# Turning a projection through the DMA crossbar instead of TensorE, and splitting the last store, in a Linformer attention and max-out feed-forward kernel

## Chip, cores, metric

One core of one Trainium2 chip. The metric is the device time of one execution in microseconds (us), the median of several; most executions of a kernel agree within 0.3%.

## The reference, cut to what matters

```python
# q, k, v: (batch 8, heads 8, seq 1024, head_dim 64); E, F: (64, 1024)
k_proj = np.einsum('ks,bhsd->bhkd', E, k)        # 64 x 64 per head
v_proj = np.einsum('ks,bhsd->bhkd', F, v)
scores = q @ k_proj.transpose(0, 1, 3, 2) / 8    # then softmax over 64
attn_out = softmax(scores) @ v_proj
x = attn_out.transpose(0, 2, 1, 3).reshape(8192, 512)
out = np.maximum(x @ w1, x @ w2) @ w_out         # w1, w2: 512 x 1024; w_out: 1024 x 512
```

The feed-forward part is computed with Strassen-like products, two units of seven products per batch. The attention of batch b is laid between the products of batch b-1, at numbered slots (14 per batch).

## The kernel before

Each engine works off its instructions in program order and waits on semaphores; the scheduler inserts the waits. kp is k's projection (64 x 64 per head) and kpt its transpose, which the scores need; "to turn" is to transpose, and "through the crossbar" means by `dma_start_transpose`.

```python
def step_kv(t, h0=0, h1=H, which="kv", att=False):     # k's and v's projection: 16 matmuls (L180)
    kv_ps = att_banks()[:, 0, :] if att else mm_bank()
    ...
    eng(out=fl(t["kp"]), in_=kv_ps[0:KP, 0:n])                              # ACT
    ...
    nc.vector.tensor_copy(out=fl(t["vp"][KP:128]), in_=kv_ps[KP:128, 0:n])
    nc.vector.tensor_copy(out=fl(t["vp"][0:KP]), in_=kv_ps[KP:128, 0:n])

def step_kpt(t, h0=0, h1=H, att=False):                # each head turned twice, to rows 0-63 and 64-127
    kpt_ps = att_banks(FP16)[:, 0, :] if att else mm_bank(FP16)
    for h in range(h0, h1):
        for r in range(2):
            nc.tensor.transpose(out=kpt_ps[r * D : (r + 1) * D, ...], in_=t["kp"][:, h, :], ...)
    nc.vector.tensor_copy(out=t["kpt"][:, h0:h1, :]..., in_=kpt_ps[...])

def step_qt_dma(t, h0=0, h1=H):                        # q is turned by the crossbar already
    nc.sync.dma_start_transpose(out=t["qt"][:, h0:h1]..., in_=t["q"][:, h0:h1]...)

def load(t, n, src, b, h0, h1, c0=0, c1=NC):           # float32 in HBM to 16 bits in SBUF
    nc.gpsimd.dma_start(out=t[n][...], in_=src[b, h0:h1]...)
...
# batches 3 to 7; step_sc (scores) reads kpt and qt
at(b - 1, -11, 0, new_attn, t)
at(b - 1, -11, 0, step_qt_dma, t, 0, H // 2)
at(b - 1, -11, 0, step_qt_dma, t, H // 2, H)
at(b - 1, -9, 0, step_kv, t, 0, H, "kv", True)
at(b - 1, -9, 0, loads, b + 1, "v", "q", "k")
at(b - 1, -8, 0, step_kpt, t, 0, H, True)
plan = "sc0 -7, da0 -6, sc1 -4, da1 -3, sc2 -1, da2 0, sc3 2, da3 3"
```

k, q and v share four buffers, so the next loads wait until the q transposes and the projection have freed three of them.

The softmax here doesn't subtract the row's maximum and nothing guards it: scores larger than these inputs give would overflow.

## Time and profile before

| | before |
|---|---|
| time, median | 347.74 us (3 runs), 347.49 us (4 runs, beside the changed kernel) |
| span of the profiled run | 345.4 us |
| TensorE busy, clock granted | 96%, 0.996 |
| projection to projection, batches 3 to 7 | 37.94 us |
| last matmul's end to the end of the span | 4.9 us |

The first row is the metric; the others are from one profiled execution. The period is read from the first matmul of the projection (line L180) of successive batches. The lines of the page are in the prediction.

### The profile page before, as it was taken

To read this page: it belongs to the slowest core of one execution; us is meant where nothing else is said; L and a number is where in the kernel's file an instruction comes from. 1 tells how busy PE (TensorE), PEld (TensorE's weight loads), DVE (VectorE), ACT (ScalarE), POOL (GpSimd) and SP (SyncE) were. 2 spreads that over 40 slices of the span, in tenths; PEclk is the share of its full clock that TensorE was granted. 3 is DMA by queue.
4 is the path that set the end of the run, shared out by engine and by line. 5 is a ranking of instruction groups with operands and counts; after the bars stand their busy time and mean duration, and the time that the engine had idled before them with its cause. 6 is when DMAs were issued, how large, how long until landed. Compare 5 with 4: busy or idle time off the path is not lost.

```text
span 345.4 us, 7094 instructions
## 1 busy us (share of the span) xinstructions
PE 332.9 (96%) x2979; PEld 233.5 (68%) x2979; DVE 232.4 (67%) x394; ACT 218.7 (63%) x325; POOL 31.5 (9%) x43
## 2 busy tenths in 40 slices
PE   8988999999999999999999999999999999999994
PEld 4543444434476777777777777777777777888883
DVE  1367717534787778686769778686869777777561
ACT  2437222773896778668884777668875788654541
POOL 8433002011103000120012000100000000000000
PEclk9999999999999999999999999999999999999998
DMA  8999999999998999799669949891923030303033
GB/s 154 200 197 201 207 207 193 238 159 260 174 205 183 195 208 250 109 191 193 173 114 181 222 122 172 150 200 20 199 47 123 2 121 2 121 5 123 0 123 121
DMA packets 65232, 52.36 MB, mean 152 GB/s; under 512 B 26160, under 2 KB 56880, under 8 KB 65200
## 3 DMA queue, kind: packets, MB, share of 16 engines
q0 software_dynamic: 31312, 28.31, 53.7%
q1 hardware_dynamic: 33888, 23.60, 25.2%
q8 instruction: 23, 0.38, 0.4%
q14 instruction: 9, 0.07, 0.1%
HBM read 57.15 MB, written 16.78 MB: 214 GB/s over the span
## 4 chain that ended last, share of the span: by engine, by line
PE 75%; DVE 9%; ACT 6%; DMA 6%; POOL 2%; issue 1%; DVEq 0%; ACTq 0%; POOLq 0%
PE mm_ps L630 31%; PE mm_ps L552 21%; PE mm_ps L385 5%; DMA big<-in_moe_w_dram 4%; PE mm_ps L359 4%; PE att_ps L265 4%; PE att_ps L180 3%; DVE big L496 2%; PE att_ps L241 2%; DVE xt_sb L279 2%; ACT ld_sb L272 2%; DVE gt_sb L567 2%; PE mm_ps L425 2%; ACT ld_sb L275 2%; PE mm_ps L520 2%
## 5 line engine op out<-in xcount | busy, mean ns | idle before, releaser
L506 ACT COPY p_sb<-mm_ps 128x512 f32<-128x512 f32 x160 | 89.1, 592 | 44.0 <-PE mm_ps L630 29.6
L630 PEld LDWEIGHTS <-big 128*128 128x128 f16 x672 | 65.7, 98 | 8.1 <-DVE big L496 0.5
L630 PE MATMUL mm_ps<-T_sb,big 128*128 128x256 f16 x504 | 61.6, 273 | 0.3 <-DVE big L496 0.3
L279 DVE TENSOR_TENSOR xt_sb<-att_ps,ld_sb 128x1024 f16<-128x1024 f32 x28 | 34.2, 1221 | 29.2 <-ACT ld_sb L275 29.1
L567 DVE TENSOR_TENSOR gt_sb<-mm_ps,p_sb 128x512 f16<-128x512 f32 x52 | 35.8, 689 | 22.4 <-PE mm_ps L552 22.4
L552 PEld LDWEIGHTS <-big 128*128 128x128 f16 x416 | 38.9, 98 | 12.7 <-issue 8.5
L552 PE MATMUL mm_ps<-big 128*128 128x256 f16 x312 | 43.7, 273 | 0.3 <-DVE gt_sb L567 0.3
L552 PEld LDWEIGHTS <-wd_sb 128*128 128x128 f16 x312 | 28.2, 98 | 13.8 <-issue 10.7
L630 PEld LDWEIGHTS <-gt_sb 128*128 128x128 f16 x336 | 32.7, 98 | 4.2 <-DVE gt_sb L570 0.2
L630 PE MATMUL mm_ps<-wo_sb,gt_sb 128*128 128x256 f16 x224 | 33.7, 273 | 0.0
L552 PE MATMUL mm_ps<-xt_sb,wd_sb 128*128 128x256 f16 x208 | 31.0, 273 | 2.3 <-DVE gt_sb L567 2.3
L249 ACT ACTIVATE ex_sb<-att_ps 128x1024 f16<-128x1024 f32 x28 | 28.9, 1031 | 4.2 <-PE att_ps L241 4.2
L272 ACT ACTIVATE ld_sb<-att_ps 128x1024 f32<-128x1024 f32 x28 | 28.9, 1030 | 3.5 <-PE att_ps L265 3.5
L275 ACT ACTIVATE ld_sb<-ld_sb 128x1024 f32<-128x1024 f32 x28 | 30.0, 1070 | 0.4
L646 DVE TENSOR_TENSOR o_sb<-mm_ps,p_sb 128x512 f32<-128x512 f32 x28 | 19.3, 689 | 12.1 <-PE mm_ps L630 12.1
L630 PE MATMUL mm_ps<-m_sb,xt_sb 128*128 128x256 f16 x112 | 21.4, 273 | 0.0
L102 POOL DMA_DIRECT2D v_sb<-in_v_dram x9 | 7.7, 863 | 145.1 <-DMA qt_sb<-q_sb 120.8
L570 DVE TENSOR_SCALAR gt_sb<-gt_sb 128x512 f16<-128x512 f16 (+1 forms) x52 | 19.1, 367 | 1.8
L496 DVE TENSOR_TENSOR big<-gt_sb 128x1024 f16<-128x1024 f16 x28 | 19.2, 685 | 0.9
L602 ACT ACTIVATE gt_sb<-mm_ps 128x512 f16<-128x512 f32 x26 | 15.6, 599 | 4.7 <-PE mm_ps L552 4.7
L630 PEld LDWEIGHTS <-xt_sb 128*128 128x128 f16 x168 | 16.4, 98 | 1.9
L567 DVE TENSOR_TENSOR gt_sb<-p_sb 128x512 f16<-128x512 f32 x26 | 17.7, 681 | 0.0
(94 smaller groups left out, 455.4 us busy)
## 6 DMA issues: line engine op xcount, KB each, us to landing
out_dram<-o_sb SPq DMA_DIRECT2D x28, 512.0 KB, 3.1
k_sb<-in_k_dram POOLq DMA_DIRECT2D x7, 1024.0 KB, 18.2
v_sb<-in_v_dram POOLq DMA_DIRECT2D x7, 1024.0 KB, 9.9
q_sb<-in_q_dram POOLq DMA_DIRECT2D x7, 1024.0 KB, 13.6
big<-in_moe_w_dram POOLq DMA_DIRECT2D x8, 256.0 KB, 14.3
out_dram<-o_sb SPq DMA_DIRECT2D x8, 256.0 KB, 4.6
k_sb<-in_k_dram POOLq DMA_DIRECT2D x2, 512.0 KB, 7.8
v_sb<-in_v_dram POOLq DMA_DIRECT2D x2, 512.0 KB, 12.5
```

What stands on the lines that cost most here:

```text
L249: nc.scalar.activation(out=ex, in_=sc_ps, func=ACTF.Exp, scale=scale)
L272: nc.scalar.activation(out=ld, in_=dn_ps, func=ACTF.Ln)
L275: nc.scalar.activation(out=ld, in_=ld, func=ACTF.Exp, scale=-1.0)
L279: nc.vector.tensor_tensor(out=t["xt"][:, p, :, :], in0=at_ps, in1=ld, op=ALU.mult)
L385: nc.tensor.matmul(out=op_ps, lhsT=lhsT, rhs=rhs, start=(n == 0), stop=(n == NFB + NDC - 1),)
L496: nc.vector.tensor_tensor(out=S(i), in0=x, in1=y, op=op)
L506: nc.scalar.copy(out=x, in_=bank)
L552: nc.tensor.matmul(out=bank[:, m * W : (m + 1) * W], lhsT=w_[:, n_, (2 * d + m) * 128 : (2 * d + m + 1) * 128], rhs=a[:, n_, :], start=(n ...
L567: nc.vector.tensor_tensor(out=c_blk(j, c), in0=two(x), in1=two(y), op=ALU.add)
L570: nc.vector.tensor_scalar_max(ap, ap, 0.0)
L630: nc.tensor.matmul(out=bank[:, i * CH : (i + 1) * CH], lhsT=a(c)[:, i * 128 : (i + 1) * 128], rhs=w_(c), start=(n is not None and i == 0 a ...
L646: nc.vector.tensor_tensor(out=cols(st["o", j], c), in0=two(x), in1=two(y), op=ALU.add)
```

## The change

Intent: free TensorE of the 16 small transposes per batch by sending kp through the DMA crossbar, with the projection moved a slot earlier to give the DMA time; and shorten the end by storing the last tile in small pieces as they become ready. Core of the diff (line numbers shift: L180 stays, L229 becomes L242, L241 L254, L630 L643, L650 L663):

```diff
-        t["kp"] = proj.tile([KP, H, D], FP16, tag="kp", name="kp_sb")
+        t["kp"] = proj.tile([KP, H, 2, D], FP16, tag="kp", name="kp_sb")
...
+            def finish_v():                         # runs after the next slot
+                nc.vector.tensor_copy(out=fl(t["vp"][KP:128]), in_=kv_ps[KP:128, 0:n])
+                if att:
+                    nc.vector.tensor_copy(out=kp[:, :, 1, :], in_=kp[:, :, 0, :])
+                    step_kpt_dma(t)
+                nc.vector.tensor_copy(out=fl(t["vp"][0:KP]), in_=fl(t["vp"][KP:128]))
...
+    def step_kpt_dma(t):
+        nc.sync.dma_start_transpose(
+            out=t["kpt"], in_=t["kp"].rearrange("p h r d -> p (h r d)")
+        )
...
         def p4():
+            if alone:                               # the last unit of the program
+                for i in range(2):
+                    bank = product(4, ("C", i), 2 + i, (i,))
+                    ...add u2 on DVE...
+                    store(1, i, i + 1, 0, CH)       # 128 KB each; p3 has stored the other half
+                return
...
-            at(b - 1, -11, 0, new_attn, t)          # and both step_qt_dma
-            at(b - 1, -9, 0, step_kv, t, 0, H, "kv", True)
-            at(b - 1, -9, 0, loads, b + 1, "v", "q", "k")
-            at(b - 1, -8, 0, step_kpt, t, 0, H, True)
+            at(b - 1, -12, 0, new_attn, t)          # and both step_qt_dma
+            at(b - 1, -9 if b == 3 else -10, 2 if b == 3 else 0, step_kv, t, 0, H, "kv", True)
+            at(b - 1, -7, 0, loads, b + 1, "v", "q", "k")
+            if b == 3:
+                plan = "sc0 -5, da0 -4, sc1 -3, da1 -2, sc2 -1, da2 0, sc3 2, da3 3"
```

More of the change, by code (lines that the diff above doesn't have):

```diff
@@ L188, in step_kv @@
             eng = nc.vector.tensor_copy if which == "k" else nc.scalar.copy
-            eng(out=fl(t["kp"]), in_=kv_ps[0:KP, 0:n])
+            kp = t["kp"][:, h0:h1]
+            eng(out=kp[:, :, 0, :], in_=kv_ps[0:KP, 0:n].rearrange("p (h d) -> p h d", d=D))
         if both:
@@ L192, in step_kv, with step_kpt @@
         elif "v" in which:
-            nc.vector.tensor_copy(out=fl(t["vp"][KP:128]), in_=kv_ps[KP:128, 0:n])
-            nc.vector.tensor_copy(out=fl(t["vp"][0:KP]), in_=kv_ps[KP:128, 0:n])
-    def step_kpt(t, h0=0, h1=H, att=False):
-        kpt_ps = att_banks(FP16)[:, 0, :] if att else mm_bank(FP16)
+            def finish_v():
[4 more added lines that the diff above has]
+                nc.vector.tensor_copy(out=fl(t["vp"][0:KP]), in_=fl(t["vp"][KP:128]))
+            return finish_v
+    def step_kpt(t, h0=0, h1=H):
+        kpt_ps = mm_bank(FP16)
         for h in range(h0, h1):
@@ L202, in step_kpt @@
                     out=kpt_ps[r * D : (r + 1) * D, (h - h0) * KP : (h - h0 + 1) * KP],
-                    in_=t["kp"][:, h, :],
+                    in_=t["kp"][:, h, 0, :],
                     identity=ident16[:KP, :KP],
@@ L610, in cat, with product @@
             return lambda n: g[:, n] if n < NG else x[:, n - NG]
-        def product(k, name, n):
+        def product(k, name, n, part=(0, 1)):
             if n is not None:
@@ L627, in product @@
             }[k]()
-            for i in range(2):
+            for i in part:
                 for c in range(NG + NX):
@@ L633, in product @@
                         rhs=w_(c),
-                        start=(n is not None and i == 0 and c == 0),
+                        start=(n is not None and i == part[0] and c == 0),
                         stop=(c == NG + NX - 1), skip_group_check=True,
@@ L647, in add, with store @@
                 out=cols(st["o", j], c), in0=two(x), in1=two(y), op=ALU.add)
-        def store(j):
+        def store(j, i0=0, i1=2, m0=0, m1=DM):
             nc.sync.dma_start(
                 out=out.rearrange("(n p i o) m -> n o p i m", p=128, i=NI, o=2)[
-                    b, o, :, 2 * j : 2 * j + 2, :
+                    b, o, :, 2 * j + i0 : 2 * j + i1, m0:m1
                 ],
-                in_=st["o", j],
+                in_=st["o", j][:, i0:i1, m0:m1],
             )
@@ L678, in p3 @@
             add(1, 1, st["u2"], st["s5"])
+            if alone:
+                store(1, m0=CH)
         def p4():
+            if alone:
+                for i in range(2):
+                    bank = product(4, ("C", i), 2 + i, (i,))
+                    part = slice(i * CH, (i + 1) * CH)
+                    nc.vector.tensor_tensor(
+                        out=st["o", 1][:, i, 0:CH], in0=bank[:, part], in1=st["u2"][:, part],
+                        op=ALU.add,
+                    )
+                    store(1, i, i + 1, 0, CH)
+                return
             bank = product(4, "X", None)
@@ L790 @@
         else:
-            at(b - 1, -11, 0, new_attn, t)
-            at(b - 1, -11, 0, step_qt_dma, t, 0, H // 2)
-            at(b - 1, -11, 0, step_qt_dma, t, H // 2, H)
-            at(b - 1, -9, 0, step_kv, t, 0, H, "kv", True)
-            at(b - 1, -9, 0, loads, b + 1, "v", "q", "k")
-            at(b - 1, -8, 0, step_kpt, t, 0, H, True)
+            at(b - 1, -12, 0, new_attn, t)
+            at(b - 1, -12, 0, step_qt_dma, t, 0, H // 2)
+            at(b - 1, -12, 0, step_qt_dma, t, H // 2, H)
+            at(b - 1, -9 if b == 3 else -10, 2 if b == 3 else 0, step_kv, t, 0, H, "kv", True)
+            at(b - 1, -7, 0, loads, b + 1, "v", "q", "k")
             plan = "sc0 -7, da0 -6, sc1 -4, da1 -3, sc2 -1, da2 0, sc3 2, da3 3"
+            if b == 3:
+                plan = "sc0 -5, da0 -4, sc1 -3, da1 -2, sc2 -1, da2 0, sc3 2, da3 3"
         for x in plan.split(", "):
```

## The prediction

> **What bounds the kernel now.** I read the page's busy times first, then the order in time around one step that is to go, then the waits of TensorE, then the transposes' times to landing, and last the DMA share in the final microseconds. The page says which engine decides:
>
> ```profile
> span 345.4 us, 7094 instructions
> PE 332.9 (96%) x2979; PEld 233.5 (68%) x2979; DVE 232.4 (67%) x394; ACT 218.7 (63%) x325; POOL 31.5 (9%) x43
> PE 75%; DVE 9%; ACT 6%; DMA 6%; POOL 2%; issue 1%; DVEq 0%; ACTq 0%; POOLq 0%
> ```
>
> TensorE is busy 96% of the span and makes 75% of the chain that ended last; its clock is full in nearly every slice. A busy PE row alone proves little, but by the list of waits it waits for DVE about 0.5 us per batch (once, after the first head pair) and for little else. So TensorE time taken away in batches 3-7 should come off the total one for one, unless a new wait takes its place. Here is the step that goes, for batch 4, from the timeline:
>
> ```profile
> 143.31 1.23 DVE L279 TENSOR_TENSOR xt_sb<-att_ps,ld_sb 128x1024 f16<-128x1024 f32 x1 [2.29 <-ACT ld_sb L275]
> ...
> 146.75 0.58 ACT L189 CAST kp_sb<-att_ps 64x512 f16<-64x512 f32 x1 [2.51 <-PE att_ps L180]
> ...
> 147.36 0.69 DVE L193 CAST vp_sb<-att_ps 64x512 f16<-64x512 f32 x1 [0.71 <-ACT kp_sb L189]
> ...
> 148.07 0.69 DVE L194 CAST vp_sb<-att_ps 64x512 f16<-64x512 f32 x1
> ...
> 148.59 0.38 PE L630 MATMUL mm_ps<-T_sb,xt_sb 128*128 128x256 f16 x2
> ...
> 148.90 0.44 PE L201 MATMUL att_ps<-ident,kp_sb 64*64 64x64 f16 x16
> ...
> 149.27 0.61 PE L552 MATMUL mm_ps<-big,wd_sb 128*128 128x256 f16 x4
> ...
> 149.59 0.42 DVE L206 COPY kpt_sb<-att_ps 128x512 f16<-128x512 f16 x1
> ...
> 152.00 0.41 PE L241 MATMUL att_ps<-qt_sb,kpt_sb 64*64 64x512 f16 x4
> ```
>
> Columns are start, duration, engine. The 16 small transposes stand between two full-size products; the first scores (L241) need kpt 2.4 us after the copy has begun. The q transposes already go through the crossbar, from the same queue as the stores (the queue's timeline, then the qt tile's time from issue to landing):
>
> ```profile
> 128.09 2.45 SPq L650 DMA_DIRECT2D out_dram<-o_sb  x2
> 130.64 3.95 SPq L229 DMA_TRANSPOSE qt_sb<-q_sb  x1
> ```
>
> ```profile
> DMA to landing us min/median/max: 4.3/5.5/10.4
> ```
>
> The transposes start as soon as the queue's earlier store is out (130.54), eight microseconds before TensorE reaches their slot. Moving them a slot earlier in the program therefore moves nothing. Last, the end of the span, in stretches of about half a microsecond (the last two columns are the DMA engines' share, 1.00 being all sixteen, and GB/s):
>
> ```profile
> 340.40:340.90 0.50, 0.05 (x1) 0.00 (x0) 0.14 (x1) 0.41 (x1) 0.00 (x0) 1.00 0.07 29
> 340.90:341.40 0.50, 0.00 (x0) 0.00 (x0) 0.00 (x0) 0.18 (x1) 0.00 (x0) 1.00 1.00 381
> 341.40:342.00 0.60, 0.00 (x0) 0.00 (x0) 0.00 (x0) 0.00 (x0) 0.00 (x0) 1.00 1.01 365
> 342.00:342.60 0.60, 0.00 (x0) 0.00 (x0) 0.00 (x0) 0.00 (x0) 0.00 (x0) 1.00 1.03 389
> 342.60:343.20 0.60, 0.00 (x0) 0.00 (x0) 0.00 (x0) 0.00 (x0) 0.00 (x0) 0.67 0.99 386
> 343.20:343.70 0.50, 0.00 (x0) 0.00 (x0) 0.00 (x0) 0.00 (x0) 0.00 (x0) 0.50 0.87 320
> 343.70:345.40 1.70, 0.00 (x0) 0.00 (x0) 0.00 (x0) 0.00 (x0) 0.00 (x0) 0.50 0.00 0
> ```
>
> Two stores of 512 KB, issued at 339.97 and 341.10, keep all DMA engines full without a break from 340.9 to 343.6. The tail is a transfer of one megabyte at about 380 GB/s, not the latency of the last store.
>
> **What the Trainium skill says.** "VectorE: DVE Perf Modes", section "The three transpose paths", gives 390 ns for a 128x128 transpose on TensorE and 1309 ns through the DMA crossbar. The change pays only if the longer path is hidden; the trace agrees in direction (0.46 us of TensorE for all sixteen, worked out below, against 4.3 us at least to the landing of a q half). "DMA: Bandwidth & Descriptors", "Issuing engines are not separate DMA queues", says that DMAs of all issuing engines run on the same 16 engines and interleave. The trace agrees: q halves that met loads took 7.3 us (issued at 99.28) and 10.4 us (71.24), those without 4.3 to 5.3. The same page, "Rules for kernel authors", advises to issue a DMA early and wait for it late, which is what the new slots do. "Perfetto Trace Analysis", "DMA Optimizations", says that splitting may end a task sooner "If DMA engines are generally idle"; in this tail they are full, so the trace gives no ground for a gain.
>
> **The change part by part.**
>
> TensorE: the product before the transposes has its last two matmuls at 148.59 and 0.11 later; at the stream's pitch of 0.11 us (12 matmuls in 1.31 us in the chain) the next matmul was due at 148.81 and ran at 149.27. The step costs 0.46 us, mode switch included. Batches 3 and 5 show the same 0.46 (110.87 to 111.33, 186.75 to 187.21). Five batches: 5 x 0.46 = 2.3 us. Projecting k and v (L180) only moves, with its two mode switches, so it costs what it did.
>
> DVE: loses the kpt copy (0.42 us), and the second copy of v now reads SBUF in 16 bits instead of PSUM (0.69 us before; I estimate 0.25, since the 128x512 16-bit clamp in L570's group takes 0.29). It gains a half-width copy of k, also some 0.25. That is 0.6 us less per batch, beside TensorE, worth nothing by itself.
>
> The new path, batch 4, on the clock of before: the product of the new slot ends its stream at 142.49 (its 12 matmuls start at 141.18). The projection starts at 142.59, the cast of k runs from 144.57 (1.98 us later, as at 144.77 to 146.75) to 145.15. DVE takes the slot's addition and clamp first (145.1 to 146.0), then v's copy to 146.74, then k's copy to 147.0: the crossbar DMA can be issued at 147.0. SP is free, since the q transposes are over by 136.6. The scores are due at 152.00 - 0.46 = 151.54. So **4.5 us are allowed** from issue to landing.
>
> What it needs: a q half is 512 KB in 2048 rows of 256 bytes; kpt is 128 KB in 512 such rows, 32 per engine. Undisturbed, 3600 rows passed in the 5 us from 170, that is 22 ns per row and engine, so 0.7 us. First byte about 0.95 us after issue and 0.3 to 0.4 us from last byte to landing (both from the tail above). Undisturbed: 2.0 us. Beside loads: (7.3 - 1.3)/128 = 47 ns or (10.4 - 1.3)/128 = 71 ns per row, so 1.5 to 2.3 us and **2.8 to 3.6 us in all**. In batches 4 to 6 loads will be running (v from about 139.6, q and k from when the projection frees their buffers). So it should land 0.9 to 1.7 us ahead of need: hidden, with a narrow margin. In batch 7 no loads run. Batch 3 has its own plan: projection two parts later, issue behind a store near 112.3, scores two slots later near 119; margin 3 us or more. Its scores and divisions then come in consecutive slots for six slots, as batch 2's do now, where the chain shows no TensorE gap beyond the usual ones.
>
> The loads, put later in the program, start when their buffers are free (the wait list shows POOL waiting for the q transposes and for the projection). The projection is earlier, so they are not later than now.
>
> The tail: the right half of the last tile (256 KB) can be issued at about 340.6, the two 128 KB pieces at about 341.0 and 341.4 (DVE must add what PSUM accumulated before, and each issue holds SP 0.37 us). With 0.95 us to the first byte, each reaches the engines while they are still full with the one before. The same megabyte ends near 343.6. Gain **0 us**, at most 0.3.
>
> Sum: 347.74 - 2.3 - 0 = 345.4.
>
> **The rivals.** (1) kpt comes late: a wait of TensorE for the DMA replaces the transposes. For it: three batches have loads running, and a q half at its worst took 10.4 us. Against: kpt has a quarter of the rows. If it took 6 us, 1.5 us x 3 batches would cost 4.5 us and the total would be about 350. I give some lateness 25%, mostly below 1 us a batch, or 0.3 us on average. (2) The tail gains as intended, since only 128 KB comes last: 0.5 to 0.9 us, total near 344.7. Against it stand the full DMA engines; 15%. (3) Batch 3's denser plan makes ACT the bound for six slots: about 1 us once, total 346.4. Against: batch 2 does it now; 20%. (4) The projection a slot earlier loosens or tightens DVE's chain, so that the 0.5 us waits per batch vanish or double: 2 us either way; the first pair's slots are unchanged in batches 4 to 7, so about 10% each.
>
> **Range and chances.** From 345.4, and about 0.2 for the mean of the rivals, I predict 345.6 us. The low end, 344.5, is the tail working half as intended and some waits gone; the high end, 347.5, is lateness of half a microsecond in three batches with a poor batch 3. Two per cent is 7 us: no gain in sight reaches it, and a loss needs kpt later by over 3 us in three batches. Faster 0.01, same 0.97, slower 0.02.
>
> **What would show it.** In the profile after: 80 fewer transposes; the period between projections 37.94 us now and 37.5 then; kpt's issue to landing 2 us undisturbed and about 3 beside loads; no wait of the L241 group for a DMA; DMA engines full until about 343.6 minus what was saved, with no shorter tail. I am wrong if TensorE waits for kpt, if the period does not shrink by 0.46, or if the time from the last matmul to the end (4.9 us, from 340.43) shrinks by over 0.3.

## More of the kernel before

The experiments ran on three chips, each beside the kernel before on its own chip (medians 347.39 to 347.50 us).

## The result, and the profile after

375.15 us (374.48 to 376.48, 4 runs) against 347.49 us: a ratio of 1.0796, 95% interval 1.0757 to 1.0835. The prediction, 345.6 us with a range to 347.5, was wrong.

The page of the changed kernel (span, busy times, and the chain that ended last by engine and by line):

```profile
span 373.1 us, 6942 instructions
PE 338.4 (91%) x2899; PEld 235.6 (63%) x2899; DVE 231.7 (62%) x396; ACT 219.1 (59%) x324; POOL 31.6 (8%) x43
...
PE 69%; DMA 15%; DVE 7%; ACT 4%; POOL 1%; issue 1%; DVEq 0%; POOLq 0%
PE mm_ps L643 28%; PE mm_ps L565 18%; DMA kpt_sb<-kp_sb 11%; PE mm_ps L398 6%; DMA big<-in_moe_w_dram 4%; PE mm_ps L372 4%; PE att_ps L278 4%; PE att_ps L254 2%; PE att_ps L180 2%; DVE xt_sb L292 2%; PE mm_ps L438 2%; PE mm_ps L533 2%; DVE big L509 2%; ACT ld_sb L285 1%; ACT ld_sb L288 1%
```

The 80 transposes are gone (2979 matmuls to 2899), yet TensorE is "busy" 5.5 us longer, and kpt's DMA has entered the chain. The waits of TensorE and the kpt tile's time from issue to landing tell why:

```profile
PE att_ps L254 <- DMA kpt_sb<-kp_sb: 22.2, 4, 6.0
```

```profile
DMA to landing us min/median/max: 2.6/10.0/12.1
```

TensorE waited four times, 22.2 us in all: in batches 3 to 6, for 5.9, 6.0, 5.7 and 4.5 us. Batch 7, without loads, did not wait; its kpt landed in 2.6 us. The timeline of batch 4, to be read beside that of before:

```profile
154.25 0.29 DVE L197 COPY kp_sb<-kp_sb 64x512 f16<-64x512 f16 x1
154.60 1.83 SPq L220 DMA_TRANSPOSE kpt_sb<-kp_sb  x1
...
165.03 0.64 PE L254 MATMUL att_ps<-qt_sb,kpt_sb 64*64 64x512 f16 x4 [6.04 <-DMA kpt_sb<-kp_sb]
```

The DMA is issued 4.6 us after the projection's first matmul (149.97), where the prediction had 4.4. From there it takes 10.4 us, and all engines run dry behind TensorE. After the wait TensorE is slow; these are pieces of the chain in order of time (start, duration):

```profile
166.63 2.56 PE mm_ps L643 x12
...
176.28 1.31 PE mm_ps L643 x12
```

The same 12 matmuls take 2.56 us after the wait and 1.31 us ten microseconds later. The reason is the clock. Single microseconds of TensorE (start and end, length, busy time, granted clock, DMA share, GB/s):

```profile
162.00:163.00 1.00, 0.00 (x0) 0.85 1.28 159
...
165.00:166.00 1.00, 0.97 (x6) 0.50 1.15 295
...
170.00:171.00 1.00, 1.00 (x14) 1.00 0.73 119
```

The Trainium skill, "TensorE: Matmul & The Clock Gate", Part 1, says that the array falls to half its clock after an idle window of about 3.4 us and needs as long to recover; the trace agrees: the clock fell to 0.50 some 3.7 us after the wait began (158.99) and was back some 4.5 us after it ended (165.03). The products after the four waits took 2.56, 2.56, 2.32 and 2.56 us, 4.8 us more than at full clock, and smaller matmuls beside them paid as well. So 22.2 of waiting, 4.8 of slow products, less 2.3 of transposes saved, is 24.7 of the 27.7 us lost; the rest, some 3 us, I have not split; those smaller matmuls (0.64 us for batch 4's four scores, 0.41 before) and the refilling of the other engines are the likely places, not shown ones.

What the DMA engines did meanwhile is seen in single microseconds (pieces, that is single packets, then MB and time share; q0 carries GpSimd's loads, q1 what SP issues). First 156 to 157, then 161 to 162:

```profile
q0 software_dynamic: 160, 0.16, 109.3%
...
q0 software_dynamic: 158, 0.15, 91.7%
q1 hardware_dynamic: 158, 0.04, 31.2%
```

Between 154.6 and 158.4 not one row of kpt moved, and only 8 by 159. From 160 on both queues moved in about equal numbers, at most 158 rows per us where undisturbed q transposes reach over 1000. The q and k loads had been triggered at 152.48 and 153.34, just before kpt. The kernel before shows the same in its q transposes. These are 77 to 78 and 80 to 81, of the q half issued at 71.24 and the one after it:

```profile
q0 software_dynamic: 139, 0.14, 89.7%
q1 hardware_dynamic: 139, 0.04, 38.3%
...
q1 hardware_dynamic: 1048, 0.31, 131.2%
```

The load ended near 79. That half took 10.4 us to land because hardly a row moved before 76; only some 500 of its 2048 rows had moved by 79, the rest when the load was over. My prediction had divided the whole time by all the rows.

The tail of the changed kernel, in half microseconds (the last two columns again DMA share and GB/s):

```profile
368.50:369.00 0.50, 0.00 (x0) 0.00 (x0) 0.11 (x1) 0.00 (x0) 0.00 (x0) 1.00 1.04 385
...
370.00:370.50 0.50, 0.00 (x0) 0.00 (x0) 0.00 (x0) 0.00 (x0) 0.00 (x0) 1.00 0.99 342
370.50:371.00 0.50, 0.00 (x0) 0.00 (x0) 0.00 (x0) 0.00 (x0) 0.00 (x0) 0.91 0.99 344
```

The engines are full for about as long as before, and the second half, in 1 KB rows, moves at 342 instead of 380 GB/s. From the last matmul's end to the end of the span it is 5.2 us, 4.9 before.

### The profile page after: what moved, and what is told of

It is laid out like the page before. It is cut to its first block, busy times and chain, and to the rows that moved or that the text cites. A ratio compares the mean times of both kernels' runs of the same rounds, so it can differ in the third digit from the quotient of the medians.

```text
span 373.1 us, 6942 instructions
## 1 busy us (share of the span) xinstructions
PE 338.4 (91%) x2899; PEld 235.6 (63%) x2899; DVE 231.7 (62%) x396; ACT 219.1 (59%) x324; POOL 31.6 (8%) x43
## 4 chain that ended last, share of the span: by engine, by line
PE 69%; DMA 15%; DVE 7%; ACT 4%; POOL 1%; issue 1%; DVEq 0%; POOLq 0%
PE mm_ps L643 28%; PE mm_ps L565 18%; DMA kpt_sb<-kp_sb 11%; PE mm_ps L398 6%; DMA big<-in_moe_w_dram 4%; PE mm_ps L372 4%; PE att_ps L278 4%; PE att_ps L254 2%; PE att_ps L180 2%; DVE xt_sb L292 2%; PE mm_ps L438 2%; PE mm_ps L533 2%; DVE big L509 2%; ACT ld_sb L285 1%; ACT ld_sb L288 1%
## 5 line engine op out<-in xcount | busy, mean ns | idle before, releaser
L643 PEld LDWEIGHTS <-big 128*128 128x128 f16 x672 | 66.3, 99 | 8.7 <-DVE big L509 0.5
L643 PE MATMUL mm_ps<-T_sb,big 128*128 128x256 f16 x504 | 62.9, 276 | 0.3 <-DVE big L509 0.3
L565 PEld LDWEIGHTS <-big 128*128 128x128 f16 x416 | 39.9, 99 | 11.5 <-issue 6.6
L565 PE MATMUL mm_ps<-big 128*128 128x256 f16 x312 | 44.5, 276 | 0.5 <-DVE gt_sb L580 0.5
L643 PEld LDWEIGHTS <-gt_sb 128*128 128x128 f16 x336 | 33.9, 102 | 5.7 <-issue 0.6
L643 PE MATMUL mm_ps<-wo_sb,gt_sb 128*128 128x256 f16 x224 | 36.5, 288 | 0.0
L565 PE MATMUL mm_ps<-xt_sb,wd_sb 128*128 128x256 f16 x208 | 31.8, 279 | 1.8 <-DVE gt_sb L580 1.8
L254 PE MATMUL att_ps<-qt_sb,kpt_sb 64*64 64x512 f16 x112 | 12.2, 425 | 22.2 <-DMA kpt_sb<-kp_sb 22.2
L643 PE MATMUL mm_ps<-m_sb,xt_sb 128*128 128x256 f16 x112 | 22.6, 286 | 0.0
L254 PEld LDWEIGHTS <-kpt_sb 64*64 64x64 f16 x112 | 3.2, 105 | 29.6 <-DMA kpt_sb<-kp_sb 23.3
L643 PEld LDWEIGHTS <-xt_sb 128*128 128x128 f16 x168 | 17.0, 101 | 2.5
## 6 DMA issues: line engine op xcount, KB each, us to landing
v_sb<-in_v_dram POOLq DMA_DIRECT2D x2, 512.0 KB, 12.1
```

The lines of the kernel that those rows point to most:

```text
L254: nc.tensor.matmul(out=sc_ps[pos : pos + KP, e, :], lhsT=t["kpt"][o * D : (o + 1) * D, 2 * p + e, :], rhs=t["qt"][o * D : (o + 1) * D, 2 * ...
L565: nc.tensor.matmul(out=bank[:, m * W : (m + 1) * W], lhsT=w_[:, n_, (2 * d + m) * 128 : (2 * d + m + 1) * 128], rhs=a[:, n_, :], start=(n ...
L643: nc.tensor.matmul(out=bank[:, i * CH : (i + 1) * CH], lhsT=a(c)[:, i * 128 : (i + 1) * 128], rhs=w_(c), start=(n is not None and i == par ...
```

## The experiments

The theory after the result: kpt's DMA comes just behind fresh loads; it starts only after some 4 us of their pieces, then shares the engines with them row against piece. Rivals: the crossbar transpose is slow by itself; the new slots or batch 3's plan hurt; the tail hurts.

### 1. Loads held back until kpt has landed

```diff
+    def held_loads(t, b, *names):
+        nc.gpsimd.tensor_copy(out=hold[0:1, 0:1], in_=t["kpt"][0:1, 0, 0:1])
+        loads(b, *names)
...
-            at(b - 1, -7, 0, loads, b + 1, "v", "q", "k")
+            at(b - 1, -7, 0, held_loads, t, b + 1, "v", "q", "k")
```

> The changed kernel, but GpSimd reads one element of kpt before it issues the loads of the next batches (batches 3 to 7), so the loads can't start before kpt has landed. Theory (kpt is starved by the loads that are queued beside it): kpt lands 2.6 to 3 us after its issue in every batch, as in batch 7 of the changed kernel now; TensorE's wait for kpt (22.2 us now) goes to under 1 us, the clock doesn't fall, and the time is 345 to 346 us. Rival A (the transpose of 64 rows through the crossbar, or its issue, is slow by itself in the middle of the program): kpt still takes 9 to 12 us and the time stays at 373 to 376 us. Rival B (the loads, held back by some 6 to 8 us, then come too late for the q transposes or for the next projection): kpt is fast, but waits for v, k or qt appear and the time is 350 to 360 us.

Measured: 345.21 us (4 runs) against 347.41, ratio 0.9935 (0.9917 to 0.9953). kpt's landing, then the timeline of batch 4:

```profile
DMA to landing us min/median/max: 2.7/2.7/3.3
```

```profile
146.51 1.20 SPq L220 DMA_TRANSPOSE kpt_sb<-kp_sb  x1
...
149.31 0.18 POOL L756 COPY hold<-kpt_sb 1x1 f16<-1x1 f16 x1 [30.47 <-DMA kpt_sb<-kp_sb]
149.85 0.88 POOL L102 DMA_DIRECT2D v_sb<-in_v_dram  x1 [0.36 <-issue]
...
150.83 0.41 PE L254 MATMUL att_ps<-qt_sb,kpt_sb 64*64 64x512 f16 x4
```

TensorE has no wait for kpt left in its list, the clock is 0.997, and kpt issues of batches 4 to 7 follow each other by 37.46 to 37.55 us. One tiny read turns a loss of 8% into a gain of 0.65%, small, but the interval stays under 1. The theory is confirmed (one landing of 3.3 us, batch 3's behind its stores, lies over the expected 3); no load came too late (rival B).

### 2. The changed slots and tail, with TensorE turning kpt

```diff
-                    nc.vector.tensor_copy(out=kp[:, :, 1, :], in_=kp[:, :, 0, :])
-                    step_kpt_dma(t)
...
+            at(b - 1, -7 if b == 3 else -8, 0, step_kpt, t, 0, H, True)
```

> The changed kernel with its new slots, its plan for batch 3 and its tail, but kpt of batches 3 to 7 turned by TensorE again (16 transposes and a DVE copy per batch). Theory (the DMA alone costs the time; slots and tail are harmless): 347 to 348 us, the same as the kernel before, with five times 0.46 us of transposes back. Rival (the earlier projection, or batch 3's denser plan, hurts by itself): 350 us or more with TensorE waiting for ACT or DVE in batches 3 to 7.

Measured: 348.15 us (346.99 to 348.65, 4 runs), ratio 1.0012 (0.9992 to 1.0033): same as before, 0.15 us over the expected range. The slots and batch 3's denser plan cost nothing that shows. The projections of batches 4 to 7 follow each other by 37.94 us, as before; in experiment 1 by 37.46 or 37.47. The difference is the 0.46 us of the transposes.

### 3. The tail alone

The edit is the diff's `product`, `store`, p3 and p4, put into the kernel before.

> The kernel before with only the last product in two parts and the small stores. Theory (the tail is one megabyte through full DMA engines): 347.2 to 347.9 us, within 0.3 us of before, and the DMA engines full for about 2.7 us from 0.9 us after the first store's issue, as before. Rival (the end is set by the last store's own latency): 0.5 to 0.9 us faster, 346.6 to 347.0 us.

Measured: 347.58 us (6 runs), ratio 1.0011 (0.9992 to 1.003): no gain, no loss that shows, though the interval would allow a loss of up to 1 us. The DMA engines were full for about 2.9 us, from 0.9 us after the first store's issue.

### 4 to 6. Three probes: what is slow, and when

TensorE turns kpt (as in experiment 2); a DMA that nobody waits for is issued from kp at the moment of the changed kernel's, into a spare tile. The kind of DMA changes over the batches in three orders.

```diff
+        if kind == "T":                            # crossbar, 512 rows of 256 bytes
+            nc.sync.dma_start_transpose(out=spare[:, 0 : H * KP]..., in_=kp)
+        elif kind == "S":                          # plain copy, 512 pieces of 224 bytes
+            nc.sync.dma_start(out=spare[0:KP]...[:, :, 0:112], in_=kp...[:, :, 0:112])
+        elif kind == "L":                          # plain copy, 64 pieces of 2 KB
+            nc.sync.dma_start(out=spare[0:KP], in_=kp)
```

> The kernel te_slots (kpt by TensorE) with one more DMA per batch 3 to 7 at the moment at which the changed kernel issues kpt's, into a spare tile that nobody reads: batch 3 the crossbar transpose of kp (512 rows of 256 bytes), batch 4 a plain copy of 512 pieces of 224 bytes, batch 5 a plain copy of 64 pieces of 2 KB, batches 6 and 7 the transpose. Nobody waits for these, so the time should be that of te_slots within 1 us. Theory (each engine takes pieces of the two queues in turn, after a start delay of about 4 us under fresh loads): transposes of batches 3 and 6 land 9 to 12 us after issue, the small copy 8 to 11 us, the large one, with 4 pieces per engine, 4 to 6 us; batch 7, without loads, 2 to 3 us. Rival (the crossbar transpose alone suffers): both plain copies land in under 5 us, as most stores do.

> As the probe before, with the kinds in another order over the batches: batch 3 the small copy (512 pieces of 224 bytes), batch 4 the large one (64 pieces of 2 KB), batch 5 the transpose, batches 6 and 7 the small copy. Theory (kind decides only by its number of pieces, and the loads do the rest): first piece about 4 us after issue in batches 4 to 6 whatever the kind; landing 6 to 7 us for the large copy, 9 to 10.5 us for the transpose and for the small copy of batch 6, 11 to 13 us in batch 3 behind a store, 2 to 3.5 us in batch 7. Rival (the crossbar makes the transposes slow): the small copies of batches 3 and 6 land in under 7 us.

> As the probe before, third order: batch 3 the large copy (64 pieces of 2 KB), batch 4 the transpose, batch 5 the small copy, batches 6 and 7 the large copy. Theory: first piece about 4 us after issue in batches 4 to 6 whatever the kind; landing 9 to 10.5 us for the transpose of batch 4 and the small copy of batch 5, 6 to 7 us for the large copy in batch 6, 8 to 10 us in batch 3 behind a store, under 3 us in batch 7. Rival (the crossbar makes the transposes slow): the small copy of batch 5 lands some us before the transpose of batch 4 does.

Measured, us from issue to landing (T transpose, S small copy, L large copy), total times 348.14, 349.45 and 347.50 us:

| order | batch 3 (behind a store) | batch 4 | batch 5 | batch 6 | batch 7 (no loads) |
|---|---|---|---|---|---|
| first | T 12.4 | S 9.5 | L 6.7 | T 8.9 | T 3.4 |
| second | S 12.2 | L 6.5 | T 9.7 | S 8.7 | S 3.4 |
| third | L 10.0 | T 10.1 | S 10.0 | L 7.3 | L 3.0 |

From the first order's list of issues:

```profile
spare<-kp_sb SPq DMA_DIRECT2D x1, 128.0 KB, 6.7
spare<-kp_sb SPq DMA_DIRECT2D x1, 112.0 KB, 9.5
```

A plain copy of as many pieces is as late as the transpose, so the crossbar is not at fault; a copy of the same bytes in an eighth of the pieces is 3 us faster but still over 6 us. In the first order the first piece moved about 4 us after issue in batches 4 and 5, whatever the kind. Several expected landings were missed, none by more than 0.7 us: in the first order T 12.4 and 8.9 (9 to 12 expected), L 6.7 (4 to 6) and T 3.4 in batch 7 (2 to 3); in the second S 8.7 in batch 6 (9 to 10.5); in the third L 7.3 in batch 6 (6 to 7) and 3.0 in batch 7 (under 3). The second order's time is 1.3 us over experiment 2's, where 1 us was expected; it is one run.

### 7. kpt in four DMAs of two heads

```diff
+        for p in range(NP2):
+            x = proj.tile([128, 2, KP], FP16, tag=f"kpt2_{p}", name="kpt2_sb")
+            nc.sync.dma_start_transpose(
+                out=x, in_=t["kp"][:, 2 * p : 2 * p + 2].rearrange("p h r d -> p (h r d)"))
```

> The changed kernel with kpt turned in four DMAs of two heads each (128 rows of 256 bytes), each into its own tile, so that the first scores wait for the first two heads alone. Theory (a start delay of about 4 us beside fresh loads, then about 150 rows per us in turn with the loads): the first DMA of batches 4 to 6 lands 5.5 to 6.5 us after issue, in place of 9 to 10.4, against 4.4 us allowed, so TensorE waits 1 to 2 us in batches 3 to 6 each (4 to 8 us in all, 22.2 now), and the time is 350 to 357 us. Rival (the whole transfer is held up until the load queue drains, so the first piece is as late as the last): TensorE still waits 4 to 6 us per batch and the time stays above 366 us.

Measured: 367.9 us (4 runs), ratio 1.0605 (1.0567 to 1.0642). The waits of TensorE:

```profile
PE att_ps L260 <- DMA kpt_sb<-kp_sb: 15.3, 4, 4.4
```

The first piece of batch 4 landed 7.7 us after issue, not 5.5 to 6.5. It too began after 4 us, but then moved only 54 and 62 rows in its first two microseconds, not 150. So my time was missed (350 to 357), and the rival's limit of 366 was passed, though not for the rival's reason: TensorE's wait did fall by 6.9 us, and the first piece came before the load's end. A quarter of the rows saves 2.7 of 10.4 us; the start delay is the larger part. Splitting is no cure. Each of the four also held SP for about 1.2 us even without loads (5.0 us for four in batch 7), as long as the one of 512 rows.

### 8. Only q's and k's loads held back

```diff
+        loads(b, "v")
         nc.gpsimd.tensor_copy(out=hold[0:1, 0:1], in_=t["kpt"][0:1, 0, 0:1])
-        loads(b, *names)
+        loads(b, "q", "k")
```

> The kernel gated, but the v load isn't held back: it may start when the q transposes have freed its buffer (about 139.5 on the clock of the kernel before), only the q and k loads wait for kpt. Theory: in batches 4 to 6 kpt meets the last third of one load only and lands 3.5 to 5.5 us after issue, in batch 3 it meets a whole fresh load and lands after 7 to 10 us; TensorE waits 0 to 1 us in batches 4 to 6 and at most 2 us in batch 3; the time is 345 to 348 us. Rival (only the q and k loads, triggered just before kpt, hold it up; an older load doesn't): no wait at all, all landings 3 to 3.5 us, and the same time as gated within 0.5 us.

Measured: 350.9 us (4 runs), ratio 1.0105 (1.0078 to 1.0133). That is above the expected 345 to 348. The only wait for kpt is batch 3's, 4.7 us: there v's load had been triggered 3 us before kpt's issue, and kpt, behind two stores, took 10.6 us (behind the same stores but without a load it took 3.3 in experiment 1). In batches 4 to 7 it took 2.7 to 2.9 us. There v's load was seven microseconds old. In batch 4, in the microsecond of issue (154 to 155), 203 load pieces moved, and in the next

```profile
q1 hardware_dynamic: 297, 0.08, 46.9%
q0 software_dynamic: 58, 0.05, 31.2%
```

the load ran out and kpt passed. Neither side had this right: I had batch 3 too cheap and batches 4 to 6 too dear. One fresh load, here with stores ahead of kpt as well, is enough to do the damage; the last pieces of an old one do none.

### 9. Loads triggered with kpt, just behind it

```diff
-        nc.gpsimd.tensor_copy(out=hold[0:1, 0:1], in_=t["kpt"][0:1, 0, 0:1])
+        nc.gpsimd.tensor_copy(out=hold[0:1, 0:1], in_=t["kp"][0:1, 0, 1, 0:1])
```

> The kernel gated, but GpSimd waits only for the copy after which kpt's DMA is issued, not for its landing: kpt and the three loads are then triggered side by side, kpt first, the loads' first pieces about a microsecond later. Theory (the start delay of 4 us is the load pieces that the engines have already taken on when kpt comes; after that the queues take turns): with nothing taken on before it kpt starts about 1 us after issue, then shares at some 150 rows per us, and lands 4.5 to 6 us after issue; TensorE waits 0 to 1.5 us in each of batches 3 to 6; the time is 346 to 353 us. Rival (loads go first whenever they are queued, whatever the order of arrival): landing 9 us or more, TensorE waits some 5 us per batch, time above 366 us.

Measured: 350.71 us (4 runs), ratio 1.0093 (1.0071 to 1.0116), in the expected range. The landings were not (4.5 to 6 us expected), so that the time fits is partly luck. Batch 4, kpt's issue and then v's load:

```profile
151.60 1.20 SPq L220 DMA_TRANSPOSE kpt_sb<-kp_sb  x1
152.21 0.88 POOL L102 DMA_DIRECT2D v_sb<-in_v_dram  x1 [0.31 <-issue]
```

kpt landed after 2.7 and 2.8 us in batches 4 and 6, though v's load was triggered 0.6 us after kpt's issue. It took 5.8 us in batch 5, with the same 0.6 us: there too over 460 of its rows moved in the second microsecond after issue, and only the last ones came late; why, I have not looked into. It took 9.6 us in batch 3, where two stores of 512 KB lay before it on SP's queue and the loads got in between. The waits left are 3.2 us (batch 3) and 1.5 us (batch 5). So the order of arrival decides, with little room: with the same loads a microsecond later kpt was not delayed in two batches and in part in a third. That the engines have already taken on the loads' pieces is my reading of it: by the counts of the changed kernel, of the kernel before and of the probes, 32 to 43 load pieces per engine moved between the issue of a delayed DMA and its first row. No run looks into the engines' queues.

### 10. Loads held, the old tail

The kernel of experiment 1 with the last product and store of before.

> The kernel gated with the kernel before's last product and last store, so that only the turning of k differs from before. Theory (the small stores bring nothing): the same time as gated, 344.9 to 345.6 us, 0.6 to 0.7% under before. Rival (the small stores bring some of gated's gain): 345.7 to 346.2 us.

Measured: 344.43 us (343.96 to 344.70, 6 runs) against 347.39, ratio 0.9905 (0.9887 to 0.9923): the fastest version and under the expected range, 0.8 us in the median under experiment 1 but on another chip, with intervals that overlap a little. The small stores have no part in the gain. From the kernel before this one differs not only in the turning of k, as was written, but also in the moved slots and the held loads; no run holds the loads while TensorE turns kpt. The slots alone gain nothing (experiment 2), and the shorter period is the transposes' 0.46 us, so the held loads can have a small part at most: of the 3 us gained some 2.3 are the transposes'. The half microsecond before the last of the tail, first of experiment 1 and then of this kernel:

```profile
340.50:341.00 0.50, 0.00 (x0) 0.00 (x0) 0.00 (x0) 0.00 (x0) 0.00 (x0) 1.00 1.02 348
```

```profile
340.50:341.00 0.50, 0.00 (x0) 0.00 (x0) 0.00 (x0) 0.00 (x0) 0.00 (x0) 1.00 1.02 385
```

From the first of these stores to the end it is 5.7 us with small stores (337.37 to 343.1) and 5.1 with the old ones (337.49 to 342.6). The other profiles lie nearer together: 5.4 in the kernel before (old stores), 5.5 to 5.7 in the changed kernel and experiments 2 and 3 (small ones). Experiment 3 shows no loss in the time, so a cost of some tenths is likely but not settled.

## Why the prediction was wrong, by its own steps

- **TensorE's saving, 5 x 0.46 us: right.** With the loads held, experiment 1 has 345.2 us, and the sum without rivals was 345.4; the period fell from 37.94 to about 37.5.
- **Time of issue: right.** 4.6 us after the projection's start instead of 4.4, DVE's two short copies 0.29 us each instead of 0.25.
- **Undisturbed time of kpt: a little short.** 2.6 to 2.7 us measured, 2.0 predicted; still inside the 4.5 allowed. Some 460 rows moved in their first microsecond (experiment 1), where 3600 pieces in 5 us, 100 of them not rows, had given 720.
- **"Beside loads: ... 47 ns or ... 71 ns per row, so 1.5 to 2.3 us and 2.8 to 3.6 us in all": this step failed.** It took the landing times of q halves as if loads had run beside all their rows. They met a load only for the first part of their rows. Read by the microsecond, the profile of before already had the terms: about 4 us before the first row, then some 140 rows per us, thus 3.7 us for 512, and about a microsecond to landing: 9 us. Measured: 8.9 to 10.4 in batches 4 to 6, 12.1 in batch 3.
- **Not seen at all: the loads start just before kpt does.** The projection frees the buffers of two of them, and they were triggered 1 and 2 us before kpt was issued. I noted that they are "not later than now" and took contention as one more load in flight; experiments 8 and 9 show that fresh loads ahead of kpt are the bad case.
- **Rival 1 was the right one, at the wrong size.** Named at 25% and "mostly below 1 us a batch", it came at 4.5 to 6.0 us in four batches. That waits of this length also halve TensorE's clock was missing: 4.8 us in the four products alone. A slower kernel had been given a chance of 0.02.
- **Batch 3's margin "3 us or more": wrong**, for the same reason, with a store ahead.
- **The tail, no gain: right**, for the reason given (full engines); its end came 0.3 us later rather than up to 0.3 earlier. **Batch 3's plan and the moved slots: harmless**, as said (experiment 2).

## What to carry to other kernels

A mean taken over a transfer that met contention for a part of its time says little about one that meets it for all of its time; look at the queue microsecond by microsecond before scaling. A place later in the program does not hold back an engine that has nothing else to do: if loads are to come after a short urgent DMA, give their engine something to wait for, here a read of one element of what the DMA writes. And moving work off the bound engine pays only while its replacement lands in time; a late one costs the wait and then the clock.

## What the Trainium skill lacked or had wrong

- "DMA: Bandwidth & Descriptors", "Issuing engines are not separate DMA queues": it says that DMAs of all engines interleave; no page has that one issued just behind fresh GpSimd loads starts only after some 4 us (154.6 to 158.4 here). A 128 KB transfer of 512 rows took 2.6 us alone and 8.9 to 10.4 us so.
- The same page, "Latency and other measured facts", has about 600 ns to the first byte of a DMA from SP. Undisturbed stores and transposes here showed 0.95 to 1.0 us from the start of the issue; beside fresh loads it is the 4 us above.
- The same page has no cost of issuing a small crossbar transpose between SBUF tiles from SP: about 1.2 us of the queue's time undisturbed, the same for 128 rows of 256 bytes as for 512.
- "Perfetto Trace Analysis", "DMA Optimizations", has no figure for splitting while the DMA engines are full: here it gave nothing (ratio 1.0011), and rows of 1 KB moved at 338 to 348 GB/s where rows of 2 KB mostly moved at 365 to 397.
